# Read-outs and updates in a pair's last step, features formed in PSUM as a minimum, and another order of the mixer's tiles

## The chip, the core and the metric

The kernel runs on one NeuronCore of a Trainium2 chip. Its engines are TensorE (PE, with its weight loads shown apart as PEld), VectorE (DVE), ScalarE (ACT), GpSimd (POOL) and SyncE (SP), which here issues all DMAs in one queue. The metric is the device time of one execution in microseconds (us); lower is better. The median before is that of three runs.

## The reference

Two kinds of layer alternate over x of 2048 rows and 640 columns, in float32: attention (A), mixer (B), attention, mixer, each added to x after a layernorm. Cut to what matters:

```python
def _A_ref(x, wq, wk, wv, wo, beta):        # 32 heads of 20, 4 segments of 512 rows
    phi = lambda t: jnp.where(t > 0, t + 1.0, jnp.exp(t))
    for s in range(N):                      # M, z: the memory of the segments before
        logits = jnp.einsum("bhqd,bhkd->bhqk", qs, ks) * scale + mask   # keys at or before the query
        p = _softmax(logits, axis=-1)
        a_dot = jnp.einsum("bhqk,bhkd->bhqd", p, vs)
        pq = phi(qs)
        num = jnp.einsum("bhld,bhde->bhle", pq, M)
        den = jnp.einsum("bhld,bhd->bhl", pq, z)[..., None] + 1e-6
        o = g * num / den + (1.0 - g) * a_dot
        pk = phi(ks)
        M = M + jnp.einsum("bhld,bhle->bhde", pk, vs)
        z = z + jnp.einsum("bhld->bhd", pk)
    return o @ wo

def _B_ref(x, w_in, w_sp, b_sp, w_out):
    z = _gelu(x @ w_in); z1 = z[..., :864]; z2 = _layernorm(z[..., 864:])
    g = jnp.einsum("ts,bsf->btf", w_sp, z2) + b_sp[None, :, None]
    return (z1 * g) @ w_out
```

The mask in the reference adds -1e9 where the column is after the row.

## The kernel before

**Numbers.** Every float32 operand of a matmul is split into two float16 parts, high and low, by a ScalarE copy and a VectorE subtraction, and each product takes three matmuls (high x high, high x low, low x high).

**Order of work.** For each of the two layers there are three stages: `phase1a` (attention), `phase1b` (the mixer's input side) and `phase2` (its spatial product and its output). TensorE's order is the order in which the code is written. The order on the other engines and in SP's queue is laid out by a planner, from its own estimate of times and from priorities: an operation goes to its engine's queue when the planner thinks that it can start, and `high_priority` puts it ahead of others that can start as well. On the chip each queue then runs strictly in that order.

**`phase1a`.** The heads go in pairs, 16 pairs in each of four segments, 64 in all, and a pair takes three steps (`run`, time t; LEAD steps come before). In each step `scores` computes one chunk of the pair's transposed logits (`es`, read by ScalarE's exponential into P) and one chunk of a later pair's logits (`mp`, read by VectorE's maximum into `mx`), each in one buffer of PSUM. The three chunks have 512, 512 and 256 columns, so a pair's last step (t % 3 == 2) is the lightest. At t % 3 == 0 the maxima of a pair are transposed (`maxes`: matmul `mtp` into the bank "ms", read by ScalarE and then by VectorE into `mr`). `pvs` does P times V for one head at t % 3 == 2 and for the other at t % 3 == 0. `cast` splits P: ScalarE makes the high part, GpSimd the low one.

Between them run the projections (`unit` for q and k, `value`, `project`), cut into pieces that `PACE` deals out in units a step. Each group of them has one of two PSUM banks "dn". When a q or k projection `ps` is done, `out` posts its evacuation to later steps: `parts` one step later (ScalarE and VectorE split it, L701 and L705, and ScalarE takes its exponential, L704), `features` a step after that (a minimum with 1 and a scale, in SBUF, L711, then max(ps, 0) plus that, L713, into `phq` or `phk`), and for keys `keys` a third step later (the split of `phk`, L722 and L723, and a transposing DMA). A step 4 later or more, `update` multiplies the keys with the values into the memory `mst` (matmuls `mup`, bank "ms"). `read` multiplies the queries' features with `mst` (matmuls `num`, bank "ms"); its `out` divides, L760 to L764, into `gm`, one step later. A layer has 18 reads (segments 1 to 3, one for each block of six heads or less) and 15 updates (segments 0 to 2, one for each block of 128 features). The bank "ms" has one buffer, so `mtp`, `num` and `mup` take turns in it. Reads stand at the steps of the list `rd`, and updates are moved on by `post` while

```python
        while free and (t % 3 == 0 or t in self.rd):
            t += 1
```

holds.

**`phase1b`.** For each of 16 tiles of 128 rows: take x1, the rows after the attention (tiles 0 to 11 were projected in `phase1a` and are loaded; tiles 12 to 15 are projected here, from x in `xt` and the attention's output in `o`, by `yp`, L272, and added, L275), layernorm, split, a transposing DMA to `th`, the two halves of w_in (`zp`, L295), gelu and layernorm of the second half (`z2`, split into `zh` and `zl`, L301 to L304), gelu of the first, stored (`z1`). Layernorm of a tile is written one tile ahead, loads two tiles ahead. The buffers of this stage are in pools, one after the other in memory: b2 (`z1`), b1 (`z2`), bx2 (`xt`), bx1 (`o`), bs (staging of w_in, layer 1 only), be2 (`x1`, `th`), be1, bw0 (first half of w_in). `g.wi[0].made` is false in layer 1 and true in layer 2, when the split weights are loaded ready-made.

**`phase2`.** It lies over the same memory: c1 (`u`, `un`, `ut`: 3456, 3584 and 3584 bytes a partition), cr (`wr`, 8192 bytes), ch (`wn`), c2, cw (w_u), cx, ctr (`wt`). For each tile of w_sp, `rows` loads 128 rows (`wr`, L353), takes their largest magnitude (L355), scales and splits them (`wn`, L365 and L366) and transposes them by DMA (`wt`, L367). `spatial` multiplies `wt` with `zh` and `zl`, over k from 0 to 15 (L378), `tail` multiplies by w_out. `rows(0)` is written first, with the priority HP. A tile of `z2` takes 3456 bytes a partition, one of `xt`, `o`, `x1` 2560, one of `z1` 3456.

Of the kernel before, what the change touches and what calls it, by code (L numbers as in the profile page):

```python
# [19 lines left out]
L = S // NSEG  # L20
# [214 lines left out]
def phase1b(g, o_d, x, x1_d, z1_d, zh, zl):  # L235
    nc, tc = g.nc, g.tc
    with ExitStack() as ctx:
        pool = lambda n, b, **k: ctx.enter_context(tc.tile_pool(name=n, bufs=b, reuse_waits="tile", **k))
        p2, p1, px2, px1, sp = pool("b2", 2), pool("b1", 3 if g.wi[0].made else 1), pool("bx2", 2), pool("bx1", 1), pool("bs", 2)

# [41 lines left out]
        def xn_t(xn):  # L282
            th = pe2.tile([128, 2, KD, 128], F16, tag="th", name="th")
            hl = pe1.tile([128, 2, D], F16, tag="xnhl", name="xnhl")
            split_t(g, hl, th, xn)
            return th[:, 0], th[:, 1]
# [19 lines left out]
        def z1_half(t, zp):  # L306
            z1 = p2.tile([128, FH], F32, tag="z1", name="z1")
            nc.scalar.activation(z1.rearrange("p (n c) -> p n c", n=2), zp[:, :, :FHH], AF.Gelu_apprx_tanh, scale=g.zi[0])
            nc.sync.dma_start(z1_d[t], z1)

        with tc.high_priority(offset=HP2):
            a = load(0)
            xn = attn_out(0, *a)
            a = load(1)
            th = xn_t(xn)
        for t in range(NT):
            if t + 1 < NT:
                xn = attn_out(t + 1, *a)
            z2_half(t, w_in_half(1, *th))
            if t + 2 < NT:  # L320
                a = load(t + 2)
            th1 = xn_t(xn) if t + 1 < NT else None
            z1_half(t, w_in_half(0, *th))
            th = th1
# [197 lines left out]
class Attention:  # L522
# [23 lines left out]
    def post(self, k, f, free=False):  # L546

        if self.now is None:
            f()
            return  # L550
        t = self.now + max(k, 1)
        while free and (t % 3 == 0 or t in self.rd):
            t += 1
        self.later.setdefault(t, []).append(f)
# [137 lines left out]
    def out(self, nm, s, m, ps):  # L692

        g, nc = self.g, self.nc
        q = nm == "q"
        ph = []

        def parts():
# [8 lines left out]
            if feature:  # L707
                self.soon(lambda: features(e))

        def features(e):  # L710
            nc.vector.tensor_scalar(e, e, 1.0, g.gq if q else g.gk, ALU.min, ALU.mult)  # L711
            ph.append((self.u4 if q else self.u1).tile([128, L], F32, tag=f"ph{nm}", name=f"ph{nm}"))
            nc.vector.scalar_tensor_tensor(ph[0], ps, 0.0, e, ALU.max, ALU.add)  # L713
            if q:
                self.phq[m] = ph[0]
                self.held["q", m] = s
            else:
                self.soon(keys)

        def keys():  # L720
            hl = self.u2.tile([128, 2, L], F16, tag="hl", name="phl")
            nc.scalar.mul(hl[:, 0], ph[0], g.sig)  # L722
            nc.vector.scalar_tensor_tensor(hl[:, 1], ph[0], g.sig, hl[:, 0], ALU.mult, ALU.subtract)  # L723
            pk = self.u2.tile([128, 2, 4, 128], F16, tag="pk", name="pk")
# [218 lines left out]
    def run(self, nseg=NSEG):  # L943
# [5 lines left out]

        rd = [(G * s + 9 * m - 5 + c0 // 2, s, m, c0) for s in range(1, nseg) for m in range(NU) for c0 in range(0, len(UH[m]), 6)]  # L950
        self.rd = {t for t, _, _, _ in rd}
# [8 lines left out]
        U, V = 6480, 4530  # L960
        PACE = (-LEAD, 2400), (0, 720), (51, 1150), (128, 1250), (END + G, 0)
        order = "02 03 v4 04 v5 v6 v7 10 11 12 13 14 v8 v9 v10 v11 20 21 p0 22 23 24 v12 v13 v14 v15 30 31 p1 32 p2 33 p3 34 p4 p5 p6 p7 p8 p9 p10 p11".split()
# [16 lines left out]
        for c in order:  # L979
# [13 lines left out]
            else:  # L993
# [3 lines left out]
                for r in range(i, i + 1 + (i % NU < NU - 1)):  # L997
                    assert r < NU or beg > G * (r // NU) + 9 * (r % NU) - 4 + (3 if r % NU == 4 else 0), (s, m, r, beg)
                assert step(acc + w) < G * s + 9 * m - LEAD - 3, (s, m, step(acc + w))
# [150 lines left out]
```

## Time and profile before

| | |
|---|---|
| median of 3 runs | 2553.36 us (2547.65 to 2554.88) |
| the profiled execution | 2541.92 us, of which the profile's span is 2540.2 us |
| attention, layers 1 and 2 | about 91 to 698 and 1365 to 1946 us of the span |
| mixer's input side, layers 1 and 2 | about 698 to 906 and 1946 to 2136 us |
| spatial part, layers 1 and 2 | about 913 to 1310 and 2154 to 2540 us |
| busy share | PE 89%, PEld 53%, DVE 57%, ACT 45%, POOL 37% |

A row of the profile names the line of the code, the engine, the operation, the tile written and the tiles read, with partitions x elements and type. In brackets or after a bar stands the idle time of the engine just before, and what ended it ("<-DVE mr L892": the VectorE operation of line 892 that writes `mr`). A busy TensorE is one with a matmul in its pipeline. The granted clock is 1.00 at full speed.

### The profile page before, as it was taken

To read this page: it belongs to the slowest core of one execution; us is meant where nothing else is said; L and a number is where in the kernel's file an instruction comes from. 1 tells how busy PE (TensorE), PEld (TensorE's weight loads), DVE (VectorE), ACT (ScalarE), POOL (GpSimd) and SP (SyncE) were. 2 spreads that over 40 slices of the span, in tenths; PEclk is the share of its full clock that TensorE was granted. 3 is DMA by queue.
4 is the path that set the end of the run, shared out by engine and by line. 5 is a ranking of instruction groups with operands and counts; after the bars stand their busy time and mean duration, and the time that the engine had idled before them with its cause. 6 is when DMAs were issued, how large, how long until landed. Compare 5 with 4: busy or idle time off the path is not lost. (4 is left out here: it accounts for less than half of the span.)

```text
span 2540.2 us, 50727 instructions
## 1 busy us (share of the span) xinstructions
PE 2248.7 (89%) x20682; PEld 1335.2 (53%) x20682; DVE 1451.8 (57%) x2766; ACT 1141.3 (45%) x1388; POOL 946.9 (37%) x728
## 2 busy tenths in 40 slices
PE   3787787899889989999997778879998997999998
PEld 2354454556545545555554445455664553555555
DVE  8667777676655455544336766766766443454431
ACT  3287676677643232212125766657765222211210
POOL 3176676788621000000004767667875100000000
PEclk9999999999999999999999989889999998999999
DMA  6823543434553478766446243342445335577652
GB/s 201 204 62 82 153 117 98 97 91 118 142 161 87 113 209 197 186 162 168 98 117 140 70 104 77 98 97 68 122 125 143 100 98 162 140 190 174 144 143 63
DMA packets 502506, 325.00 MB, mean 128 GB/s; under 512 B 408512, under 2 KB 443456, under 8 KB 497152
## 3 DMA queue, kind: packets, MB, share of 16 engines
q1 hardware_dynamic: 502272, 321.76, 49.2%
q8 instruction: 162, 2.65, 0.4%
q14 instruction: 72, 0.59, 0.1%
HBM read 148.25 MB, written 85.34 MB: 92 GB/s over the span
## 5 line engine op out<-in xcount | busy, mean ns | idle before, releaser
L882 POOL TENSOR_TENSOR PL<-P,PH 128x1280 f16<-128x1280 f32 x248 | 651.7, 2628 | 227.2 <-ACT PH L881 180.7
L871 DVE TENSOR_REDUCE mx<-mp 128x2 f32<-128x1024 f32 (+3 forms) x512 | 408.8, 816 | 180.3 <-PE mp L827 178.5
L378 PE MATMUL gp<-zh,wt 128*128 128x432 f16 x2048 | 466.0, 348 | 27.6 <-DMA wt<-wn 27.6
L864 ACT ACTIVATE P<-es,sc 128x1024 f32<-128x1024 f32 (+1 forms) x384 | 371.2, 967 | 203.4 <-PE es L827 202.3
L378 PEld LDWEIGHTS <-wt 128*128 128x128 f16 x3072 | 301.8, 98 | 289.5 <-DMA wt<-wn 28.9
L881 ACT CAST PH<-P 128x1280 f16<-128x1280 f32 x256 | 320.7, 1254 | 19.6 <-PE pv L908 13.0
L295 PEld LDWEIGHTS <-th 128*128 128x128 f16 x1920 | 188.3, 98 | 167.0 <-issue 4.0
L378 PE MATMUL gp<-zl,wt 128*128 128x432 f16 x1024 | 272.5, 348 | 0.0
L393 POOL MEMSET un<- 128x64 f16 x32 | 4.9, 152 | 672.2 <-DMA ut<-un 618.1
L205 POOL TENSOR_TENSOR lnrs<-lnve,mhalf 128x1 f32<-128x1 f32 x96 | 58.8, 621 | 459.9 <-DVE lnve L204 443.8
L855 PEld LDWEIGHTS <-qk 60*128 60x128 f16 (+1 forms) x2048 | 89.6, 95 | 255.6 <-issue 153.3
L855 PE MATMUL mp<-qk 60*128 60x512 f16 (+3 forms) x1024 | 140.3, 311 | 72.4 <-DVE mx L871 70.3
L355 DVE TENSOR_REDUCE am<-wr 128x1 f32<-128x2048 f32 x32 | 73.1, 2286 | 216.6 <-DMA wr<-in_B_w_sp_dram 216.6
L381 ACT ACTIVATE u<-gp,bsp,un 128x864 f32<-128x864 f32 x32 | 34.2, 1070 | 357.9 <-PE gp L378 345.6
L630 PE MATMUL vps<-wvh,xt 128*128 128x320 f16 x640 | 160.7, 317 | 22.4 <-DMA xt<-xnhl 12.9
L407 PE MATMUL cyp<-wuh,ut 128*128 128x320 f16 (+1 forms) x896 | 166.5, 303 | 8.8 <-DMA ut<-un 8.8
L908 PE MATMUL pv<-vs,PL 128*128 128x41 f16 x2560 | 165.0, 182 | 7.9 <-POOL PL L882 7.3
L908 PE MATMUL pv<-vs,PH 128*128 128x41 f16 x2560 | 168.5, 183 | 3.8 <-DVE ab L924 2.0
L827 PEld LDWEIGHTS <-big 64*128 64x128 f16 x3072 | 142.9, 97 | 52.9 <-issue 3.8
L407 PEld LDWEIGHTS <-ut 128*128 128x128 f16 (+1 forms) x1344 | 132.7, 99 | 66.2 <-DMA ut<-un 10.0
L855 PE MATMUL es<-qk 64*128 64x512 f16 (+3 forms) x1024 | 136.5, 303 | 27.2 <-ACT P L864 21.8
L908 PEld LDWEIGHTS <-PH 128*128 128x128 f16 x2560 | 142.6, 97 | 22.6 <-ACT PH L881 3.1
(181 smaller groups left out, 4152.4 us busy)
## 6 DMA issues: line engine op xcount, KB each, us to landing
wr<-in_B_w_sp_dram SPq DMA_DIRECT2D x32, 1024.0 KB
qk<-st SPq DMA_DIRECT2D x256, 120.0 KB
x<-x SPq DMA_DIRECT2D x56, 320.0 KB
z<-z SPq DMA_DIRECT2D x32, 432.0 KB
cz<-z SPq DMA_DIRECT2D x32, 432.0 KB
xt<-in_A_x_dram SPq DMA_DIRECT2D x32, 320.0 KB
st<-qhl SPq DMA_DIRECT2D x40, 256.0 KB
st<-khl SPq DMA_DIRECT2D x40, 256.0 KB
```

The lines of the kernel that those rows point to most:

```text
L295: nc.tensor.matmul(zp[:, n, :FHH], a[:, k, :], b[:, k, c:c + FHH], start=(k == 0 and j == 0), stop=(k == KD - 1 and j == 2))
L355: nc.vector.tensor_reduce(am, wr, AX.X, ALU.max, apply_absolute_value=True)
L378: nc.tensor.matmul(gp[:, n, :FHH], wt[:, k // 8, a, k % 8, :], b[:, k, n * FHH:(n + 1) * FHH], start=(k == 0 and j == 0), stop=(k == NT - ...
L407: nc.tensor.matmul(yp[:, n, :320], a[:kn[k], k, :], b[:kn[k], k, n * 320:(n + 1) * 320], start=(k == 0 and j == 0), stop=(k == KO - 1 and ...
L630: nc.tensor.matmul(ps, a[:, k, c], b[:, k, n * 320:(n + 1) * 320], start=(i == 0), stop=(i == 14))
L827: nc.tensor.matmul(out, g.big[r, 64 - 64 * s:192 - 64 * s], mk, start=False, stop=s == 1, skip_group_check=True)
L855: nc.tensor.matmul(out[:, h, o:o + w], a[r, ac], b[r, bc], start=o == 0, stop=False, skip_group_check=True)
L864: nc.scalar.activation(P[:, :, 512 * c:512 * c + ew], es[:, :, :ew], AF.Exp, scale=g.esc)
L871: nc.vector.tensor_reduce(self.mx[m][:, :, i], mp[:, :, o:o + w], AX.X, ALU.max)
L881: nc.scalar.copy(PH, P[:, h])
L882: (nc.gpsimd if h == 0 or n < self.N - self.TAIL else nc.vector).tensor_tensor(PL, P[:, h], PH, ALU.subtract)
L908: nc.tensor.matmul(pv[:, i, h, :], x[:, c:c + 128], v[:, j, h0 + h, :], start=(j == 0 and x is PH), stop=(j == i and x is PL), skip_group_ ...
```

## The change

It has four parts.

1. In `phase1b` the tiles are taken in the order 0 to 7, 12 to 15, 8 to 11, so that the four with projections stand in the middle. In layer 2, `z2` has one buffer instead of three and `o` three instead of one.
2. `features` goes. In `parts`, VectorE replaces `ps` in PSUM by max(ps, 0) + c (c is the scale of 1), and takes the minimum of that and the exponential times c: for t > 0 the exponential is not below t + 1, for t <= 0 it is not above 1. For a query the result goes to `phq`, for a key back into `ps`. `keys` comes one step later instead of two, and reads PSUM. The tile `phk` (2048 bytes) is gone.
3. Reads move one step later, from t % 3 == 1 to the pair's last step, and updates are allowed only there, at a step that has no read.
4. `PACE` deals out 700 units a step up to step 53 instead of 720 up to step 51.

```diff
-        p2, p1, px2, px1, sp = pool("b2", 2), pool("b1", 3 if g.wi[0].made else 1), pool("bx2", 2), pool("bx1", 1), pool("bs", 2)
+        p2, p1, px2, px1, sp = pool("b2", 2), pool("b1", 1), pool("bx2", 2), pool("bx1", 3 if g.wi[0].made else 1), pool("bs", 2)
...
+        ts = [*range(NWO - 4), *range(NWO, NT), *range(NWO - 4, NWO)]
         with tc.high_priority(offset=HP2):
-            a = load(0)
-            xn = attn_out(0, *a)
-            a = load(1)
+            a = load(ts[0])
+            xn = attn_out(ts[0], *a)
+            a = load(ts[1])
             th = xn_t(xn)
-        for t in range(NT):
-            if t + 1 < NT:
-                xn = attn_out(t + 1, *a)
+        for i, t in enumerate(ts):
+            if i + 1 < NT:
+                xn = attn_out(ts[i + 1], *a)
             z2_half(t, w_in_half(1, *th))
-            if t + 2 < NT:
-                a = load(t + 2)
-            th1 = xn_t(xn) if t + 1 < NT else None
+            if i + 2 < NT:
+                a = load(ts[i + 2])
+            th1 = xn_t(xn) if i + 1 < NT else None
             z1_half(t, w_in_half(0, *th))
...
-        while free and (t % 3 == 0 or t in self.rd):
+        while free and (t % 3 < 2 or t in self.rd):
...
             if feature:
-                self.soon(lambda: features(e))
-
-        def features(e):
-            nc.vector.tensor_scalar(e, e, 1.0, g.gq if q else g.gk, ALU.min, ALU.mult)
-            ph.append((self.u4 if q else self.u1).tile([128, L], F32, tag=f"ph{nm}", name=f"ph{nm}"))
-            nc.vector.scalar_tensor_tensor(ph[0], ps, 0.0, e, ALU.max, ALU.add)
-            if q:
-                self.phq[m] = ph[0]
-                self.held["q", m] = s
-            else:
-                self.soon(keys)
+                one = g.gq if q else g.gk
+                nc.vector.tensor_scalar(ps, ps, 0.0, one, ALU.max, ALU.add)
+                ph = self.u4.tile([128, L], F32, tag="phq", name="phq") if q else ps
+                nc.vector.scalar_tensor_tensor(ph, e, one, ps, ALU.mult, ALU.min)
+                if q:
+                    self.phq[m] = ph
+                    self.held["q", m] = s
+                else:
+                    self.soon(keys)
...
-            nc.scalar.mul(hl[:, 0], ph[0], g.sig)
-            nc.vector.scalar_tensor_tensor(hl[:, 1], ph[0], g.sig, hl[:, 0], ALU.mult, ALU.subtract)
+            nc.scalar.mul(hl[:, 0], ps, g.sig)
+            nc.vector.scalar_tensor_tensor(hl[:, 1], ps, g.sig, hl[:, 0], ALU.mult, ALU.subtract)
...
-        rd = [(G * s + 9 * m - 5 + c0 // 2, s, m, c0) for s in range(1, nseg) for m in range(NU) for c0 in range(0, len(UH[m]), 6)]
+        rd = [(G * s + 9 * m - 4 + c0 // 2, s, m, c0) for s in range(1, nseg) for m in range(NU) for c0 in range(0, len(UH[m]), 6)]
...
-        PACE = (-LEAD, 2400), (0, 720), (51, 1150), (128, 1250), (END + G, 0)
+        PACE = (-LEAD, 2400), (0, 700), (53, 1150), (128, 1250), (END + G, 0)
```

More of the change, by code (lines that the diff above doesn't have):

```diff
@@ L695, in out @@
         q = nm == "q"
-        ph = []
         def parts():
@@ L997, in run @@
                 for r in range(i, i + 1 + (i % NU < NU - 1)):
-                    assert r < NU or beg > G * (r // NU) + 9 * (r % NU) - 4 + (3 if r % NU == 4 else 0), (s, m, r, beg)
+                    assert r < NU or beg > G * (r // NU) + 9 * (r % NU) - 3 + (3 if r % NU == 4 else 0), (s, m, r, beg)
                 assert step(acc + w) < G * s + 9 * m - LEAD - 3, (s, m, step(acc + w))
```

## The prediction

> **What bounds the kernel now.** I read the page first, then the busy time by stage, then TensorE's waits, and last the chain of work at the places that these named.
>
> ```profile
> span 2540.2 us, 50727 instructions
> PE 2248.7 (89%) x20682; PEld 1335.2 (53%) x20682; DVE 1451.8 (57%) x2766; ACT 1141.3 (45%) x1388; POOL 946.9 (37%) x728
> ```
>
> TensorE carries the kernel; no other engine is above 57%. So the question is where TensorE stands still. The stages (start:end in us, length, then PE, PEld, DVE, ACT, POOL busy with counts, clock, DMA share, GB/s), here attention and mixer of layer 1, of layer 2, and a gap before layer 2's spatial part:
>
> ```profile
> 91.00:698.00 607.00, 508.70 (x6735) 317.44 (x6732) 427.90 (x807) 415.80 (x523) 418.46 (x275) 0.95 0.43 111
> 698.00:906.00 208.00, 197.63 (x1197) 109.40 (x1194) 104.19 (x206) 67.14 (x75) 31.37 (x39) 0.98 0.45 121
> 1365.00:1946.00 581.00, 492.40 (x6666) 310.39 (x6664) 396.80 (x753) 405.41 (x500) 421.91 (x278) 0.94 0.38 98
> 1946.00:2136.00 190.00, 188.70 (x1069) 103.95 (x1069) 88.65 (x188) 55.14 (x63) 22.39 (x35) 0.98 0.36 93
> 2136.00:2155.00 19.00, 0.81 (x4) 0.28 (x3) 6.34 (x9) 3.17 (x3) 0.15 (x1) 0.60 0.96 317
> ```
>
> The mixer is full (188.7 of 190), the attention stages leave 98 and 89 us, and 18 us are empty at 2136. What ended TensorE's waits (total, times, longest):
>
> ```profile
> PE mp L855 <- DVE mx L871: 70.3, 59, 3.5
> PE num L751 <- DVE mr L892: 46.3, 26, 3.3
> PE mup L781 <- DVE mr L892: 29.5, 13, 3.8
> PE gp L378 <- DMA wt<-wn: 27.6, 3, 18.2
> ...
> PE kps L687 <- DVE phk L713: 10.8, 4, 2.9
> ```
>
> Nearly all are waits for VectorE: for the maxima of the chunk before (`mx`), for `mr`, which empties the one PSUM bank "ms" that transposed maxima, read-outs (`num`) and updates (`mup`) share, and 27.6 us for the first rows of w_sp.
>
> **Part 1, the mixer's order and its buffers.** The rows of the first spatial tile go wr load, maximum, wn, transposing load to wt. In layer 2 (chain) and at both starts (TensorE):
>
> ```profile
> 2069.26 10.95 PE zp L295 x60
> 2136.27 0.32 SPq L96
> 2137.17 7.06 DMA wr<-in_B_w_sp_dram
> 2144.26 2.30 DVE am L355
> 2149.84 4.54 DMA wt<-wn
> 913.03 0.90 PE L378 MATMUL gp<-zh,wt 128*128 128x432 f16 x2 [7.44 <-DMA wt<-wn]
> 917.91 0.53 PE L378 MATMUL gp<-zl,wt 128*128 128x432 f16 x2
> 918.28 0.89 PE L378 MATMUL gp<-zh,wt 128*128 128x432 f16 x4
> 935.00 0.54 PE L378 MATMUL gp<-zh,wt 128*128 128x432 f16 x2 [1.96 <-DMA wt<-wn]
> 2154.43 0.90 PE L378 MATMUL gp<-zh,wt 128*128 128x432 f16 x2 [18.19 <-DMA wt<-wn]
> ```
>
> The whole chain, 17.3 us, lies open in layer 2. By the tile sizes, added up in the order of the pools, wr takes bytes 10,624 to 18,816 of the stage. In layer 1 these are xt and o of the projected tiles, in layer 2 the second and third z2 and the first xt. Layer 1's queue shows it: wr is issued the moment the last projected tile has been added.
>
> ```profile
> 883.73 0.89 DVE L275 SCALAR_TENSOR_TENSOR x<-yp,sc,xt 128x640 f32<-128x640 f32 x1 [3.38 <-PE yp L272]
> 884.64 0.33 SPq L353 DMA_DIRECT2D wr<-in_B_w_sp_dram  x1
> 2119.85 0.98 ACT L301 ACTIVATE z<-zp,sc 128x864 f32<-128x864 f32 x1 [1.13 <-PE zp L295]
> 2124.90 1.06 DVE L304 TENSOR_TENSOR zl<-z,zh 128x864 f16<-128x864 f32 x1 [1.03 <-ACT zh L303]
> ```
>
> In layer 2 tile 14's z2 is free at 2125.96, but wr stands in SP's queue behind the load of w_u (L96), whose memory w_in holds until TensorE's last matmul. After the change only xt and o lie under wr in both layers (z2 ends at 10,368 with one buffer, three o end at 23,168), and both are free five tiles, 5 x 10.95 = 55 us, before the mixer's end. The chain of 17.3 us then fits with room, even for wn's second half, which lies on the x1 buffer freed some two tiles (22 us) before the end. Gain: 7.44 + 1.96 in layer 1, 18.19 in layer 2, and the slow clock after each gap: 14 matmuls took 4.88 us (913.03 to 917.91) where 0.18 us apiece makes 2.6, so 2.3 us each. Sum 32 us. Ends: 0, if another load keeps wr back, and 32.
>
> The projections themselves only move: 60 matmuls in 10.95 us per tile stay, the last tile's zl is now needed at the twelfth of sixteen k instead of the sixteenth, 12 us into the spatial tile, so nothing waits. One z2 buffer in layer 2 is free: its life, 2119.85 to 2125.96, is 6.1 us of a tile's 10.95, as in layer 1 now. The x1 stores, loads of xt and transposing loads of o keep their number and stand four iterations earlier in SP's queue, the x1 loads of tiles 8 to 11 four later; the wr load and the two wt transposes are moved ahead of the last tiles' th transposes, which have a tile's time of cover. Maximum and two splits, 2.3 + 2 x 1.28 us of VectorE, go into a stage where it is busy 88.65 of 190 us. If that cover failed, the price is one th late by these 4.9 us a layer.
>
> **Part 2, features in PSUM.** Groups (count, busy us, mean ns, idle before) and one line's spread (min/median/max):
>
> ```profile
> L711 DVE TENSOR_SCALAR eq<-eq,sc 128x512 f32<-128x512 f32 x60 | 57.3, 956 | 0.0
> L723 DVE SCALAR_TENSOR_TENSOR phl<-phk,sc,phl 128x512 f16<-128x512 f32 x30 | 35.7, 1189 | 2.3 <-ACT phl L722 2.2
> L713 DVE SCALAR_TENSOR_TENSOR phq<-qps,eq 128x512 f32<-128x512 f32 x30 | 20.7, 691 | 0.3
> L711 DVE TENSOR_SCALAR eq<-eq,sc x60: 465/838/2608, 78.3 to 1843.0; 128x512 f32<-128x512 f32 x60
> ```
>
> Operations that read a projection in PSUM take 0.69 us, all alike; the two that read only SBUF scatter up to 2.6 us. The count of operations stays; L711's successor and L723 now read PSUM. A one-input operation from PSUM to PSUM is not in the trace: ends 0.465 (the fastest L711) and 0.956 (no change); I take 0.69, the nearest row. Then 57.3 - 60 x 0.69 = 15.9, and 35.7 - 30 x 0.69 = 15.0: 30.9 us less VectorE. How much of it TensorE sees depends on how often a scattered one stands before `mx` or `mr`; ends 0 and 31, I take half, 15.5. The features no longer wait a step for the exponential, but their first operation stands behind L705, which needs ScalarE's split; the exponential is issued next to that split, so I cost the wait at nothing, and at one more ScalarE operation of L705's size each (60 x 0.69 = 41, not in the sum) if another stands between.
>
> A key's bank is now held until L723, two more operations on it, about 2 x 0.69 = 1.4 us, against four known waits for `phk` (10.8 us): 4 x 1.4 = +5.6, ends 0 and 30 x 1.4 = 42. A query's bank is free a step earlier.
>
> **Part 3, read-outs and updates in step 3 of a pair.** One read-out that waited, one that did not, and what follows each:
>
> ```profile
> 1473.08 1.75 DVE L711 TENSOR_SCALAR eq<-eq,sc 128x512 f32<-128x512 f32 x1
> 1475.88 1.28 DVE L871 TENSOR_REDUCE mx<-mp 128x2 f32<-128x768 f32 x2
> 1477.08 0.27 DVE L892 SCALAR_TENSOR_TENSOR mr<-mtp,mr 8x128 f16<-8x128 f32 x1
> 1477.40 1.96 PE L751 MATMUL num<-mst,phq 128*128 128x126 f32 x8 [3.35 <-DVE mr L892]
> 1480.02 0.66 DVE L764 TENSOR_TENSOR gm<-num,den 128x480 f32<-128x480 f32 x1
> 1792.80 1.16 PE L751 MATMUL num<-mst,phq 128*128 128x126 f32 x8
> 1795.97 0.38 PE L687 MATMUL kps<-xt,wkl 128*128 128x512 f16 x1
> 1797.36 0.39 PE L855 MATMUL mp<-qk 60*128 60x512 f16 x2
> 1798.58 0.27 PE L889 MATMUL mtp<-ident,mx 128*8 128x128 f32 x1
> ```
>
> Today a read-out comes one step after the maxima's transpose (`mtp`), ahead of that step's projections, and waits for `mr`, which VectorE takes late. In the last step it comes after the projections, the third chunk's scores and a P.V product, which fill the wait. But `mr` stands just behind the middle chunk's `mx` (1475.88), and the third chunk's scores wait for that too: most of the wait turns into a wait for `mx`. Of 46.3 + 29.5 = 75.8 us I take a third, 25; ends 0 and 75.8. After long waits matmuls run slower: the eight of a read-out 1.96 against 1.16. About six such waits spared, with the projections behind them some 1.3 us each: 8; ends 0 and 39 x 1.3 = 51.
>
> Late next is `mtp`, which finds the bank still read by `gm`: the read-out's three VectorE operations end 1480.68, 1.3 us after the matmuls (1479.36), and TensorE has 1795.97 to 1798.58 = 2.6 us of other work before `mtp`. Covered unless VectorE is busy: 36 read-outs x 0.4 = +14; ends 0 and, with a 1.22 us `mx` and its wait for scores put first, 1.7 x 36 = 61. An update moved to the last step may start up to three steps later; its state is read only a segment later.
>
> **Part 4, pace.** By step 128 the projections have had 53 x 700 + 75 x 1150 = 123,350 units instead of 51 x 720 + 77 x 1150 = 125,270; at 1250 a step they end 1.5 steps later, some 190 of 200. The ten steps left cover it: 0. Without them, 1.5 x 2.8 us a layer.
>
> **The sum.** -32 - 15.5 + 5.6 - 25 - 8 + 14 = -60.9 us. The profiled execution took 2541.92 us (span 2540.2), so 2481; the median of the runs shown is 2553.36, 0.45% higher, and 2553 - 61 gives 2492, my forecast for a median.
>
> **Rivals.**
> (a) The attention gains nothing: each wait for `mr` becomes one for `mx`. For it: `mx` is already the largest row. 2553 - 32 = 2521.
> (b) Fp32 from PSUM costs a rate. The fastest L711 needs 0.465 us, an operation on PSUM 0.69: if the 0.465 were what matters, part 2 would lose 60 x 0.225 = 13.5 and win 15.0 back on L723, net 0; 2492 + 15.5 = 2508. The median of 838 ns speaks against it. The Trainium skill, "VectorE: DVE Perf Modes", section "Why PSUM operands drop a tier", states that an operation that doubles its rate on two SBUF read ports loses that with a PSUM operand; the trace agrees on the ends, but not on the mean.
> (c) The first spatial tile still waits, because a load placed before wr holds SP's queue: 2553 - 29.5 = 2524. Layer 2 shows just that now; against it, the memory is free so much earlier.
> (d) All of it counts: VectorE's 31 us, two thirds of the `mr` waits (50), the clock 20, no new waits: 2553 - 133 = 2420.
> (e) Slower: the "ms" bank. VectorE takes the `mx` of the next pair before the read-out's division, so `mtp` waits 1.7 us at all 36 read-outs (+61), and since `mr` is then late too, nothing of the 25 and the 8 comes: -32 - 15.5 + 5.6 + 61 = +19, 2572. It decides from about 1.4 us a read-out.
> (f) Neither hand-over nor attention moves: 2553.
>
> **How the numbers follow.** Chances: forecast 0.39, (a) 0.20, (b) 0.06, (c) 0.10, (d) 0.10, (e) 0.09, (f) 0.06. The forecast's own range is 2470 to 2510; with (a), (b), (c) and a share of (d) it becomes 2445 to 2532. Faster by over 0.3% (about 8 us, what a measurement can tell): 0.39 + 0.20 + 0.06 + 0.10 + 0.10 = 0.85; same 0.06; slower 0.09.
>
> **What would show it.** Part 1: no TensorE wait for wt over 1 us, the wr load issued some 50 us before the mixer's end. Part 2: the feature operations at 0.65 to 0.75 us without scatter. Part 3: `num` and `mup` almost gone from the waits for `mr`, a new small row of `mtp` waiting for `gm`, and `mx` shrunk or grown: if it has grown by what `mr` lost, (a) holds. The forecast fails if wr is still behind w_u, if `mtp <- gm` is over 40 us, or if `phk`'s row grows by tens.

## The result, and the profile after

The changed kernel took 2469.86 us (median of 4 runs, 2468.54 to 2476.31) against 2550.51 us (4 runs, 2545.8 to 2554.88) of the kernel before on the same chip: a ratio of 0.9689, 95% interval 0.9662 to 0.9716, or 81 us less. The prediction said 2492 in a range of 2445 to 2532. The sum came out near by luck, not by its own terms: the mixer's order, which was to bring the most, brought nothing, and the attention brought far more, so that two errors of opposite sign largely cancelled. The profiled executions give the same picture (spans 2540.2 and 2466.8 us).

The busy time of the changed kernel's engines, and what ended TensorE's waits (total us, times, longest):

```profile
PE 2224.2 (90%) x20682; PEld 1317.4 (53%) x20682; DVE 1431.5 (58%) x2766; ACT 1137.3 (46%) x1388; POOL 937.1 (38%) x728
```

```profile
PE mp L855 <- DVE mx L871: 55.0, 72, 3.2
PE es L855 <- ACT P L864: 34.7, 44, 2.2
PE kps L689 <- DVE phl L723: 25.6, 6, 8.3
PE gp L380 <- DMA wt<-wn: 23.8, 4, 12.2
...
PE es L855 <- DMA qk<-mr: 10.2, 7, 3.5
```

The rows for `mr` (46.3 of the read-outs, 29.5 of the updates) are gone but for 0.5, and `mx` has shrunk with them, from 70.3 to 55.0. Three rows have grown: the key projections that wait for their bank (10.8, now 25.6), the scores behind P and behind their queries (21.8 and 3.6, now 34.7 and 10.2). The wait for wt has hardly moved (27.6, now 23.8). Together the rows for `mr`, `mx`, the key projections and the scores fall by 57 us.

Busy time by stretch shows where that ends up (start:end, length, PE, PEld, DVE, ACT, POOL with counts, clock, DMA share, GB/s). First before, then after, cut in each layer at the first scores, at the last chunk of logits for a maximum (below: the attention's end; the last pair's own scores still follow it), at the first projection of the mixer and at the first spatial product:

```profile
97.00:687.00 590.00, 492.38 (x6577) 308.02 (x6577) 420.58 (x795) 407.28 (x513) 412.29 (x270) 0.95 0.42 111
687.00:698.50 11.50, 10.82 (x148) 6.85 (x144) 5.27 (x10) 8.32 (x10) 6.68 (x6) 0.76 0.41 81
698.50:913.00 214.50, 197.13 (x1181) 108.90 (x1177) 108.61 (x210) 70.31 (x79) 30.87 (x39) 0.97 0.46 126
1335.00:1923.00 588.00, 498.19 (x6576) 310.94 (x6576) 405.11 (x779) 400.17 (x501) 412.71 (x276) 0.94 0.40 101
1923.00:1933.50 10.50, 8.58 (x145) 5.92 (x140) 5.41 (x10) 8.10 (x10) 8.04 (x6) 1.00 0.50 89
1933.50:2154.40 220.90, 197.52 (x1181) 108.99 (x1177) 100.97 (x203) 64.39 (x72) 30.11 (x40) 0.95 0.42 121
```

```profile
100.50:652.00 551.50, 486.76 (x6556) 302.40 (x6556) 409.17 (x790) 403.48 (x510) 407.49 (x270) 0.96 0.44 116
652.00:670.00 18.00, 13.83 (x202) 9.04 (x202) 11.11 (x18) 12.40 (x14) 9.69 (x8) 0.91 0.46 113
670.00:878.50 208.50, 195.36 (x1144) 107.32 (x1140) 105.85 (x206) 67.04 (x76) 27.60 (x37) 0.99 0.46 128
1301.00:1836.00 535.00, 473.57 (x6557) 296.60 (x6556) 386.68 (x763) 395.87 (x499) 408.33 (x274) 0.99 0.41 105
1836.00:1866.80 30.80, 14.83 (x252) 10.41 (x251) 16.94 (x34) 16.01 (x17) 17.23 (x15) 0.82 0.49 156
1866.80:2073.50 206.70, 194.51 (x1080) 106.44 (x1080) 94.39 (x193) 58.23 (x66) 18.98 (x30) 0.96 0.45 113
```

Read as differences: the two attention stretches lose 38.5 and 53.0 us, 91.5 in all. Of these 61 are idle time (187.4 before, 126.2 after: length less PE) and 30 are busy time of TensorE on about the same count of matmuls, at a clock of 0.96 and 0.99 instead of 0.95 and 0.94. The two stretches behind them must be read together, because work moves across the cut between them: in layer 1 the mixer is 6.0 us shorter and the stretch ahead of it 6.5 longer (226.0 us in sum before, 226.5 after); in layer 2 it is 14.2 shorter and 20.3 longer (231.4 before, 237.5 after). So these stretches, from which the sum expected most of its first 32 us, give back 6.6. Another 6.9 are given back in the last spatial part (385.6 us before, 392.5 after) and some 3.5 before the first scores; no term of the sum had these.

### The profile page after: what moved, and what is told of

Read it like the earlier page. It is cut to its first block, busy times and chain, and to the rows that moved or that the text cites. A ratio compares the mean times of both kernels' runs of the same rounds, so it can differ in the third digit from the quotient of the medians.

```text
span 2466.8 us, 50722 instructions
## 1 busy us (share of the span) xinstructions
PE 2224.2 (90%) x20682; PEld 1317.4 (53%) x20682; DVE 1431.5 (58%) x2766; ACT 1137.3 (46%) x1388; POOL 937.1 (38%) x728
## 4 chain that ended last, share of the span: by engine, by line
PE 56%; DVE 10%; ACT 10%; DMA 9%; issue 5%; SPq 3%; POOL 3%; ACTq 0%; DVEq 0%; POOLq 0%
PE gp L380 16%; PE zp L295 13%; PE cyp L409 6%; ACT PH L881 3%; ACT P L864 3%; PE vps L632 3%; PE pv L908 3%; DVE mx L871 3%; DMA wr<-in_B_w_sp_dram 2%; PE kps L689 2%; PE mp L855 2%; PE qps L689 2%; PE yps L665 2%; PE es L855 2%; POOL PL L882 2%
## 5 line engine op out<-in xcount | busy, mean ns | idle before, releaser
L380 PE MATMUL gp<-zh,wt 128*128 128x432 f16 x2048 | 466.6, 348 | 23.8 <-DMA wt<-wn 23.8
L881 ACT CAST PH<-P 128x1280 f16<-128x1280 f32 x256 | 320.5, 1253 | 19.2 <-PE pv L908 12.8
L409 PE MATMUL cyp<-wuh,ut 128*128 128x320 f16 (+1 forms) x896 | 166.8, 303 | 11.9 <-DMA ut<-un 11.9
L855 PE MATMUL es<-qk 64*128 64x512 f16 (+3 forms) x1024 | 134.3, 298 | 47.3 <-ACT P L864 34.7
L295 PE MATMUL zp<-wi1h,th 128*128 128x432 f16 x640 | 150.2, 349 | 8.8 <-DMA th<-xnhl 8.8
```

What stands on the lines that cost most here:

```text
L295: nc.tensor.matmul(zp[:, n, :FHH], a[:, k, :], b[:, k, c:c + FHH], start=(k == 0 and j == 0), stop=(k == KD - 1 and j == 2))
L380: nc.tensor.matmul(gp[:, n, :FHH], wt[:, k // 8, a, k % 8, :], b[:, k, n * FHH:(n + 1) * FHH], start=(k == 0 and j == 0), stop=(k == NT - ...
L409: nc.tensor.matmul(yp[:, n, :320], a[:kn[k], k, :], b[:kn[k], k, n * 320:(n + 1) * 320], start=(k == 0 and j == 0), stop=(k == KO - 1 and ...
L855: nc.tensor.matmul(out[:, h, o:o + w], a[r, ac], b[r, bc], start=o == 0, stop=False, skip_group_check=True)
L881: nc.scalar.copy(PH, P[:, h])
```

## Experiments

All ratios are to the kernel before, run beside each kernel on its chip; "us" is the ratio's distance from 1 times 2551. Two kernels are compared by this column, unless the text gives their medians.

| kernel | median us | ratio, 95% interval | us |
|---|---|---|---|
| part 1 alone | 2556.21 | 1.0010 (0.9998 to 1.0023) | +3 |
| part 2 alone | 2506.30 | 0.9820 (0.9795 to 0.9846) | -46 |
| part 3 alone | 2479.55 | 0.9717 (0.9694 to 0.9740) | -72 |
| updates of part 3 alone | 2527.53 | 0.9910 (0.9893 to 0.9927) | -23 |
| read-outs of part 3 alone | 2485.38 | 0.9742 (0.9726 to 0.9757) | -66 |
| parts 2 and 3 | 2464.22 | 0.9668 (0.9644 to 0.9692) | -85 |
| all three (the change) | 2469.86 | 0.9689 (0.9662 to 0.9716) | -79 |
| the change, first operation in SBUF | 2483.53 | 0.9752 (0.9728 to 0.9776) | -63 |
| the change, x1 off the attention's pool | 2462.65 | 0.9667 (0.9645 to 0.9688) | -85 |
| the change, wn and wt lying free | 2434.64 | 0.9543 (0.9524 to 0.9562) | -117 |
| the same, all key features in SBUF | 2438.74 | 0.9575 (0.9554 to 0.9597) | -108 |
| the same, the first key features in SBUF | 2429.42 | 0.9524 (0.9508 to 0.9541) | -121 |
| parts 2 and 3 with pads, order of before | 2455.36 | 0.9625 (0.9609 to 0.9641) | -96 |

### Part 1 alone

```diff
-p2, p1, px2, px1, sp = pool("b2", 2), pool("b1", 3 if g.wi[0].made else 1), pool("bx2", 2), pool("bx1", 1), pool("bs", 2)
+p2, p1, px2, px1, sp = pool("b2", 2), pool("b1", 1), pool("bx2", 2), pool("bx1", 3 if g.wi[0].made else 1), pool("bs", 2)
...
+ts = [*range(NWO - 4), *range(NWO, NT), *range(NWO - 4, NWO)]
```

> Part 1 alone on the kernel before: the mixer's order and its two buffer counts, nothing in the attention. Theory, from the two traces: the load of wr now goes out some 60 us early, but the split wn sits in ScalarE's queue right behind the last tile's zh, so the transposing loads of wt still come after the mixer's last matmul; only wr and the maximum leave the open chain. Expected: layer 1's wait for wt stays at 7 us, layer 2's falls from 18 to about 12, and two to four waits for ut of some 2.7 us come in behind it: 5 to 15 us less in all, about 2541. Rival A (the sum of the prediction): the order alone is worth 32 us and something in the attention's change took it back: 2519. Rival B: the order is worth nothing, because what the second gap loses comes back as waits for ut: 2551.

Measured: +3 us, no difference. Rival B's number, but by another way than it named. TensorE's wait at layer 2's hand-over fell from 18.2 to 12.2 us as the theory said; the stretch from the attention's end to the first projection, before 10.5 us (row 1923.00:1933.50), took 30.7:

```profile
1927.00:1957.70 30.70, 13.45 (x243) 9.74 (x237) 15.51 (x31) 16.02 (x17) 15.50 (x15) 0.72 0.49 155
1957.70:2163.00 205.30, 193.18 (x1080) 106.03 (x1080) 94.41 (x193) 58.22 (x66) 19.01 (x30) 0.97 0.44 114
```

205.3 instead of 220.9 in the mixer, 30.7 instead of 10.5 ahead of it: the order pays 20.2 us in layer 2 to gain 15.6. Part of both is the same work on the other side of the cut, as the mixer's first projections now stand behind the last scores; the sum of the two, 236.0 instead of 231.4, is 4.6 us longer although the wait for wt is 6 us shorter.

### Parts 2 and 3 alone, and together

Part 2 alone is the change's `parts` and `keys`, part 3 alone the two lines below with the pace and the bound on the order of jobs; the third kernel has both.

```diff
-                nc.vector.tensor_scalar(e, e, 1.0, g.gq if q else g.gk, ALU.min, ALU.mult)
+                nc.vector.tensor_scalar(ps, ps, 0.0, one, ALU.max, ALU.add)
```
```diff
-        while free and (t % 3 == 0 or t in self.rd):
+        while free and (t % 3 < 2 or t in self.rd):
-        rd = [(G * s + 9 * m - 5 + c0 // 2, ...
+        rd = [(G * s + 9 * m - 4 + c0 // 2, ...
```

> Part 2 alone on the kernel before: features in the projection's own step, max and add written back to PSUM, min taken from PSUM; read-outs, updates and mixer as before. Theory: VectorE loses 23 us of busy time, of which a third or so reaches TensorE, and the key's bank is held longer, which costs 15 us in waits of the key projections: between -15 and +10 us, taken at -5, 2546. Rival A: the scattered SBUF-only operations were what made mx and mr late, so this part carries the attention's gain: 30 us or more less, with num<-mr and mup<-mr much smaller in the trace, 2520 or less. Rival B: the part costs by itself because of the key bank: 15 us more, 2566.

> Part 3 alone on the kernel before, with the pace that its order of jobs needs: read-outs and updates in the third step of a pair; features and mixer as before. Theory: the waits for mr (75.8 us) go nearly whole, with mx about as before (70) and mtp<-gm under 5: 50 to 65 us less, about 2493. Rival A (the prediction's third): 25 to 35 us less, about 2520, because the scattered feature operations still keep mx late and the waits move there: mx grows by 30 us or more. Rival B: it only works together with the shorter feature operations: under 15 us less.

> Parts 2 and 3 together on the kernel before, with the pace; the mixer's order and buffers as before. Alone, part 2 was worth 46.7 us, part 3 73.4 us and part 1 nothing (-3.2). Theory: parts 2 and 3 take away the same waits for mr, so together they are worth no more than some 80 us, and part 1 is worth nothing beside them either, as its gain of 12 to 15 us in the mixers is lost where layer 2's mixer starts: 2470, within 8 us of the changed kernel. Rival A: part 1 is worth its 15 us or more here, and this kernel takes 2485. Rival B: part 1 costs here too, more than it gains: 2455.

Measured: -46, -72 and -85 us. Part 2 alone met its rival A: it was worth nine times what the theory gave it. Part 3 alone did a little more than the theory, and rival A of it (a third) is out. Together they are worth 85, not 118: each removes waits that the other removes too. TensorE's waits in part 2 alone, then in part 3 alone:

```profile
PE mp L853 <- DVE mx L869: 56.7, 63, 3.5
PE num L749 <- DVE mr L890: 35.2, 28, 2.9
...
PE mup L779 <- DVE mr L890: 7.5, 6, 2.3
```

```profile
PE mp L855 <- DVE mx L871: 87.6, 90, 3.2
```

With shorter features `mr` is in time for three quarters of what the updates waited (29.5 to 7.5) and a quarter of the read-outs (46.3 to 35.2). With the read-outs and updates moved, no row of `num` or `mup` for `mr` is left, and 17 of the 76 us turn up at `mx` (70.3 to 87.6): a quarter, where the prediction had let two thirds turn up there. With both, `mx` is at 58.3. The third kernel is 6 us ahead of the changed kernel, with intervals that overlap (0.9644 to 0.9692 and 0.9662 to 0.9716): part 1 brings nothing beside the others either.

### Updates and read-outs, each alone

The updates alone are this line; the read-outs alone are the other line of part 3, with the pace and the bound on the order.

```diff
-        while free and (t % 3 == 0 or t in self.rd):
+        while free and (t % 3 < 2 or t in self.rd):
```

> One half of part 3 alone on the kernel before: updates go only into the last step of a pair; read-outs stay where they were, a step after the maxima's transpose. Theory: each kind of product saves its own wait for mr: mup's 29.5 us go, num's 46.3 stay: 20 to 30 us less, about 2522. Rival A: most of part 3's 73 us hang on the updates, because an update also holds VectorE's next mr back: 50 us less or more. Rival B: the waits move to num: under 10 us less.

> The other half of part 3 alone on the kernel before: read-outs one step later, in the last step of a pair, with the pace and the bound on the order that this needs; updates still in the second or third step where no read-out stands. Theory: num's 46.3 us go, mup's 29.5 stay, and as the read-outs now fill the third step, more updates stand in the second, so mup's wait grows by up to 10: 35 to 45 us less, about 2510. Rival A: nearly all of part 3 is in the read-outs: 65 us less or more, 2480. Rival B: the waits move to mup: 15 us less or less.

Measured: -23 us, as the theory said, and -66 us, its rival A. TensorE's waits, first with only the updates moved (no row of `mup` for `mr` is left), then with only the read-outs (none of `num`):

```profile
PE mp L855 <- DVE mx L871: 86.3, 74, 3.1
PE num L751 <- DVE mr L892: 42.6, 25, 3.3
```

```profile
PE mp L855 <- DVE mx L871: 66.1, 69, 3.6
...
PE mup L781 <- DVE mr L892: 21.3, 14, 3.6
```

Each move removes its own wait and leaves most of the other's. What differs is `mx` (70.3 before): with the updates moved it takes back 16 of their 29.5 us, with the read-outs moved it falls by 4. So the 17 us that part 3 hands to `mx` come with the updates; the read-outs' wait did not turn into one for `mx`. The read-outs brought 66 us for 46.3 of waiting, and 62 of them lie in the two attention stretches: TensorE stands idle there for 149.4 us instead of 187.4, 38 less and not 46, since the wait for P takes some back (30.1 us instead of 21.8), and it is busy for 966.6 instead of 990.6, 24 less for the same products, at a clock of 0.96 and 0.98 instead of 0.95 and 0.94.

### The first feature operation back in SBUF

```diff
-                nc.vector.tensor_scalar(ps, ps, 0.0, one, ALU.max, ALU.add)
+                nc.vector.tensor_scalar(e, e, 1.0, one, ALU.min, ALU.mult)
-                nc.vector.scalar_tensor_tensor(ph, e, one, ps, ALU.mult, ALU.min)
+                nc.vector.scalar_tensor_tensor(ph, ps, 0.0, e, ALU.max, ALU.add)
```

> The changed kernel with the features in the same step as now, but formed as before: minimum and multiply on the exponential in SBUF, then max and add from PSUM (keys still end in their own bank). One difference: the first operation works in SBUF. Theory: this operation scatters again (mean 0.9 us, up to 2 us and more, where the one in PSUM takes 0.75 at every time), VectorE is busy 8 to 13 us longer, and mx is late more often: 5 to 15 us more than the changed kernel, 2480. Rival A: what counted was that the features come in the step of their projection and the key's split reads PSUM; the place of the first operation is worth nothing: 2470. Rival B: half of these operations then take 0.47 us and no longer wait on nothing else: 5 to 10 us less, 2462.

Measured: 16 us slower than the changed kernel, the theory's upper end; the intervals are apart (0.9728 to 0.9776 and 0.9662 to 0.9716). So the memory of this one operation matters, not only the step it stands in; it is worth no less than what part 2 still adds to part 3 (13 us). The wait for `mx`, 55.0 us in the changed kernel, has grown by 12:

```profile
PE mp L855 <- DVE mx L871: 67.3, 74, 3.2
```

The operation's spread (min/median/max ns), here and in the changed kernel:

```profile
L711 DVE TENSOR_SCALAR eq<-eq,sc x60: 465/630/2047, 77.8 to 1790.9; 128x512 f32<-128x512 f32 x60
```

```profile
L711 DVE TENSOR_SCALAR kps<-kps,sc x30: 737/750/754, 77.8 to 1634.1; 128x512 f32<-128x512 f32 x30
L711 DVE TENSOR_SCALAR qps<-qps,sc x30: 736/749/751, 188.8 to 1769.8; 128x512 f32<-128x512 f32 x30
```

What makes it scatter stands on another engine. Rows of VectorE and GpSimd of this kernel, in order of time:

```profile
1475.59 2.62 POOL L882 TENSOR_TENSOR PL<-P,PH 128x1280 f16<-128x1280 f32 x1
1476.62 1.87 DVE L711 TENSOR_SCALAR eq<-eq,sc 128x512 f32<-128x512 f32 x1
```

GpSimd's split of P ends at 1478.21, the feature operation at 1478.49, 0.28 us later. The same 0.28 to 0.29 us stand behind nearly every split of P that such an operation met halfway, however early it began. I set every such operation of the kernel before beside GpSimd's operations in its trace: 25 of the 60 had none beside them for more than 4 ns and took 465 to 478 ns; the 34 covered for half their time or more took 470 to 2608, 1320 on average. The split of the key's feature with both inputs in SBUF (L723 before) does the same: 734 to 752 ns for the 10 with nothing beside them, up to 2359 for the others. With an operand in PSUM nothing of it is seen: 33 operations of the changed kernel's L711 lay wholly under GpSimd's and took 736 to 751. No run takes GpSimd's work away; the cause rests on these ends and on the operation's move.

The Trainium skill, "SBUF — State Buffer", section "SBUF: two separate sides", says that VectorE and GpSimd share one pair of SBUF ports, and that for a VectorE operation in a two-port mode or with two SBUF inputs it is "an **exclusive lock**, not a bandwidth split", held for a whole instruction by whichever starts first. These rows agree for the operation on `eq`: one that meets the 2.62 us split of P lasts until 0.28 us after the split's end, and the one that began 0.16 us ahead of a split (kernel before, at 301.9 us) took 0.47 us.

### x1 off the attention's pool

```diff
+pad = 168 if g.wi[0].made else 0
-xt = px2.tile([128, D], F32, tag="xt", name="xt")
+xt = px2.tile([128, D + pad], F32, tag="xt", name="xt")[:, :D]
```

> The changed kernel with xt 168 floats wider in layer 2's mixer, and nothing else: that moves x1 from byte 162,272 to 163,616, just past the attention's last pool but one (158,496 to 163,616); wn still lies on x1. Theory: in layer 2 the first loads of x1 waited for that pool (issued at 1849.71, 14 us after the attention's last scores; before, 19 us ahead of them), so the first tile of the mixer no longer fills the attention's end. With the pad the first x1 is loaded before the last scores, the first projections of w_in lie between the last P.V products, the wait of 7.3 us for th goes, and layer 2's stretch from last scores to first spatial tile is 10 to 15 us shorter; the wait for wt stays near 12 us: 10 to 16 us less than the changed kernel, about 2457. Rival A: the late start is the order's own (the queues hold the loads for another reason), and nothing moves: 2470. Rival B: an earlier start is given back in full at the hand-over to the spatial part.

Measured: 6 us less than the changed kernel, half of what the theory said, with intervals that overlap. The trace shows the mechanism and where the rest stayed. SP's queue, first load of x1 of layer 2 in the changed kernel, then with the pad, and then the padded kernel's stretches:

```profile
1849.71 0.83 SPq L254 DMA_DIRECT2D x<-x  x2
```

```profile
1823.94 0.39 SPq L255 DMA_DIRECT2D x<-x  x1
```

```profile
1843.00:1861.00 18.00, 14.19 (x206) 9.16 (x205) 10.99 (x18) 12.55 (x15) 9.69 (x7) 0.91 0.57 177
1861.00:2068.70 207.70, 193.39 (x1141) 106.93 (x1137) 98.15 (x199) 60.85 (x69) 26.49 (x37) 0.98 0.44 115
```

The changed kernel loads x1 14 us after the attention's end, the padded one 19 us ahead of it. From there to the first spatial product it takes 225.7 us instead of 237.5, 11.8 less, as expected; but the attention before it took 541.5 us instead of 535.0 in this build, most of it busy time of TensorE (478.5 instead of 473.6) at a clock of 0.97 instead of 0.99. So the cause of the 30.8 us row is shown (three z2 became one and o three, which put x1 of layer 2 at byte 162,272, on a pool of the attention that ends at 163,616), its worth only as 6 to 12 us.

### wn and wt lying free

```diff
+pad = 480 if g.wi[0].made else 256
-xt = px2.tile([128, D], F32, tag="xt", name="xt")
+xt = px2.tile([128, D + pad], F32, tag="xt", name="xt")[:, :D]
-xo = px.tile([128, 2, 320], F32, tag="xo", name="xo")
+xo = px.tile([128, D + 32], F32, tag="xo", name="xo")[:, :D].rearrange("p (n c) -> p n c", n=2)
```

> The changed kernel, with its buffers shifted by padding and nothing else: xt of the projected tiles is 480 (layer 2) or 256 (layer 1) floats wider and xo 32 floats, so that wn (bytes 157,920 to 166,112) no longer lies on x1's buffers, and wt's first buffer no longer on w_in's. Every instruction and its operands stay. Theory: what kept the hand-over was wn's memory, not the order. wn and the two transposing loads of wt then leave the queues while the last tiles of the mixer run, TensorE has no wait for wt over 1 us in either layer: 15 to 25 us less than the changed kernel, about 2449. Rival A: the transposing loads still come late, because the transposes of the last tiles' th and the stores before them hold the queue or collide with them: th is late by 5 us a layer and the gain is under 8 us, 2464. Rival B: the time comes back behind the hand-over as waits for ut and cx1, because the first spatial tiles then catch up with the load of w_u: under 5 us less, 2467.

Measured: 35 us less than the changed kernel by the medians (2434.64 against 2469.86; 37 by the ratios), more than the theory's 15 to 25, and 4.6% less than the kernel before. The pad also moves x1 off the attention's pool, so the 11.8 us of the experiment before are part of it; whether wn's buffer or wt's held the chain was not told apart. The hand-over in layer 2, all engines, in the changed kernel:

```profile
1996.83 0.34 SPq L355 DMA_DIRECT2D wr<-in_B_w_sp_dram  x1
...
2060.26 0.91 ACT L303 CAST zh<-z 128x864 f16<-128x864 f32 x1 [3.13 <-DVE z L211]
2061.08 2.18 ACT L367 ACTIVATE wn<-wr,ivw 128x1024 f16<-128x1024 f32 x2
2061.61 0.32 SPq L96 DMA_DIRECT2D wuh<-w_uh  x1
2064.36 9.50 SPq L369 DMA_TRANSPOSE wt<-wn  x2
2073.81 0.90 PE L380 MATMUL gp<-zh,wt 128*128 128x432 f16 x2 [12.22 <-DMA wt<-wn]
```

wr is loaded 64 us ahead of the mixer's end, as predicted, and its maximum taken at 2002.2; then nothing of the chain follows until wn, which stands in ScalarE's queue right behind the last zh. With the pads, the waits for wt are gone from TensorE's list, and the first spatial product comes without one:

```profile
1976.93 0.34 SPq L356 DMA_DIRECT2D wr<-in_B_w_sp_dram  x1
2032.86 3.93 SPq L370 DMA_TRANSPOSE wt<-wn  x1
...
2042.23 0.53 PE L381 MATMUL gp<-zh,wt 128*128 128x432 f16 x2
```

wn's first half now runs at 1987.5, 74 us earlier than at 2061.1. By stretches, layer 1's mixer falls from 208.5 to 200.4 and its spatial part from 422.5 to 414.5, layer 2's end of attention from 30.8 to 18.0 and its mixer from 206.7 to 195.8, the last part from 392.5 to 390.2; layer 2's attention took 543.3 instead of 535.0, with 61.7 and 61.4 us of idle time in it: the 8 us are busy time (481.6 and 473.6) at a clock of 0.97 instead of 0.99.

### The same pads without the mixer's order

```diff
-xt = px2.tile([128, D], F32, tag="xt", name="xt")
+xt = px2.tile([128, D + 256], F32, tag="xt", name="xt")[:, :D]
```

> Parts 2 and 3 with the mixer's order and buffer counts of before, and the same kind of pads (xt 256 floats wider in both layers, xo 32): wn no longer lies on x1, wt no longer on w_in, but wr still lies on buffers that the last tiles use. Without the pads this took 2464.2. Theory: order and memory are needed together in layer 2. There wr still stands behind the load of w_u and the wait of 18 us for wt stays; in layer 1, where wr is free one tile before the end, the wait of 7.4 us and the one behind it go, with the slow clock after them: 10 to 15 us less than without the pads, 2452. Rival A: the memory alone was the obstacle: 25 us less or more, 2438. Rival B: without the order the pads do nothing in either layer: 2464.

Measured: 9 us less than without the pads by the medians (2455.36 against 2464.22; 11 by the ratios), near the theory's 2452. In layer 1 the wait for wt is 1.13 us, where the kernel before has 7.44; in layer 2 it stays:

```profile
870.12 0.54 PE L378 MATMUL gp<-zh,wt 128*128 128x432 f16 x2 [1.13 <-DMA wt<-wn]
...
2064.60 0.90 PE L378 MATMUL gp<-zh,wt 128*128 128x432 f16 x2 [18.16 <-DMA wt<-wn]
```

The order alone brings nothing (+3), the pads alone 9 to 11, order and pads 32 (0.9668 to 0.9543): in layer 2 it takes both.

### The key's feature in SBUF, for all keys or for the first

On the kernel with wn and wt free:

```diff
-ph = self.u4.tile([128, L], F32, tag="phq", name="phq") if q else ps
+ph = self.u4.tile([128, L], F32, tag="phq", name="phq") if q else self.e1.tile([128, L], F32, tag="phk", name="phk")
```
and in the second kernel the new tile only while `self.now is None or self.now < 0`, else `ps`.

> The last kernel of the first set (changed kernel with its buffers shifted so that wn and wt lie free, 2434.6) with the key's feature written to SBUF instead of back into its bank, so that a key's PSUM bank is free one operation after the other instead of after its split. Theory: the waits of the key projections for that split (27.7 us, of it two of 9 us at the start of each layer's attention) fall to some 10, but the split (0.74 us from PSUM) takes up to 1.19 us from SBUF, 13 us more VectorE: 5 to 12 us less, 2427. Rival A: the start's waits are those of the queue of transposes behind them and stay, with VectorE longer: 5 us more, 2440. Rival B: no change, 2435.

> The changed kernel with its buffers shifted (2434.6), and the key's feature in SBUF only for the keys formed before the first pair; all others end in their bank. Theory: in each layer the wait of some 9 us of the key projections at the start falls to about 3, as where all keys went to SBUF (attention began at 96.6 instead of 100.8 us), and the later splits keep 0.74 us: 4 to 8 us less, 2429. Rival A: what is gained at the start is waited for by the maxima behind it: no change, 2435.

Measured: 2438.74, 4 us more than with all keys in their bank by the medians (8 by the ratios), rival A's end; and 2429.42, 5 us less, the theory's number. Both intervals overlap that of the kernel they start from (0.9554 to 0.9597, and 0.9508 to 0.9541, against 0.9524 to 0.9562), so neither difference is certain. With all keys in SBUF their wait falls (27.7 to 12.8), but the split takes 735 to 2766 ns and `mx` grows from 56.7 to 76.7:

```profile
PE mp L856 <- DVE mx L872: 76.7, 83, 3.5
...
PE kps L690 <- DVE phk L714: 12.8, 4, 5.9
```

```profile
L724 DVE SCALAR_TENSOR_TENSOR phl<-phk,sc,phl x30: 735/1392/2766, 81.4 to 1634.9; 128x512 f16<-128x512 f32 x30
```

With SBUF for the first keys alone the wait falls as far (12.8), the eight splits from SBUF take 732 to 752 ns with no GpSimd operation beside them, and `mx` grows only to 64.1: the gain stays, and about a third of the price. That kernel has the lowest median here.

## Why the prediction was right in sum and wrong in its terms

**Part 1, -32 predicted, nothing measured.** The step that failed is "The chain of 17.3 us then fits with room, even for wn's second half, which lies on the x1 buffer freed some two tiles (22 us) before the end". I had worked out wr's bytes against the buffers above it and found them free five tiles early, and they were. But a chain is only as early as its last buffer: wn was still planned behind the last tile's zh, and its transposing loads then stood behind w_u's loads, so of the chain only wr and the maximum went, 6 of the 18.2 us in layer 2; with wn's and wt's buffers moved it all went. And I had costed the moved pools at nothing outside the mixer: x1 of layer 2 slid onto a pool that the attention still used, which cost 12 us (237.5 against 225.7) at the place where the mixer's first tile used to fill the attention's end. The 32 us themselves were sized about rightly: against parts 2 and 3 without the order, order and pads together brought 32, with all 29.8 us of waiting for wt gone. That this agrees to the microsecond is chance, since the attention stretches of these builds differ by several. Rival (c), "The first spatial tile still waits", was the nearest, with another holder than the one it named.

**Part 2, -15.5 + 5.6 = -10 predicted.** On top of part 3 it brought 13 (0.9717 to 0.9668), alone 46. The durations were taken at 0.69 and came to 0.745 (L711) and 0.741 (L723), and L713 rose from 0.687 to 0.741, so VectorE lost 22.8 us instead of 30.9 (57.3 + 35.7 + 41.2 before; 44.7 + 22.2 + 44.5 after). Counting half of that time was too low by far: alone, the part brought twice the busy time that VectorE lost. I read that so, that an operation which meets GpSimd comes late just where `mx` and `mr` stand behind it in VectorE's queue; that is argued from the rows, and only the 16 us of the one operation, with 12 more of waiting for `mx`, are measured. The bank's price was +14.8 instead of +5.6 (25.6 against 10.8): not 1.4 us at each known wait, but up to 8.3 us at a layer's start. Rival (b), that fp32 from PSUM costs a rate, is right on the rate (0.745 us against 0.47 alone in SBUF) but falls on the time, with the operation put back into SBUF: 16 us slower.

**Part 3, -25 - 8 + 14 = -19 predicted.** On top of part 2 it brought 39 (0.9820 to 0.9668), alone 72. The mis-sized term is "most of the wait turns into a wait for `mx`": a quarter did, and that quarter came with the updates; with the read-outs alone `mx` fell. The +14 for `mtp` behind `gm` came to 1.2 us (1.9 with part 3 alone), so the 2.6 us of cover held and rival (e) had no ground. The clock's 8 came to some 30 us of busy time over all parts. For the attention rival (d) was nearest: its terms there make 101 us, and the two stretches lost 91.5.

**Part 4.** Its own worth was not tried: the read-outs' new place needs it. The stretch behind the attention's end is 18.0 us instead of 11.5 and 10.5 even where x1 is loaded in time, but nothing is lost by that: the mixer's first projections now stand behind the last pair's scores (layer 1: scores until 669.5 us, projection from 670.4) and not among them (before: projection from 698.5, scores until 706.3), and the mixer's own stretch is shorter by about as much. In layer 2 the stretch is 18.1 us with the read-outs alone (with the pace), 10.8 with the updates alone and 11.9 with part 2 alone; whether the read-outs or the pace moved the projections was not told apart.

So -32 that did not come and some -50 that were not foreseen left a total 20 us under the forecast. What stays open besides: why the granted clock of an attention stretch differs from build to build (0.99 and 0.97 in layer 2 for the same edit with and without pads, worth 8 us), and why the last spatial part is 6.9 us longer.

## What to carry to other kernels

An operation of VectorE that, like these two, reads and writes only SBUF may be priced by what GpSimd does at that moment, not by its fastest row: look at its spread, set the slow ones beside GpSimd's rows, and give it a PSUM operand where a bank can be spared. Before a hand-over is counted, follow every buffer of its chain to the byte, and after pools are resized do the same for the stage ahead, since the buffers that slide may fall on memory that is still in use. And parts that remove the same wait must not be added: two that brought 46 and 72 us alone brought 85 together.

## What the hardware showed that was not expected

- VectorE blocked, not slowed, by GpSimd: 0.47 us alone, up to 2.6 us beside the split of P, ending 0.28 us after it.
- An operation with one input from PSUM back to PSUM, 128x512 fp32, takes 0.745 us, at 736 to 754 ns for all 60.
- TensorE's products took less time in kernels where it waited less: in the two attention stretches 990.6 us busy and 187.4 idle before, 966.8 and 139.2 with part 3 alone, 960.3 and 126.2 after, at about the same count of matmuls. It is no strict rule: with the first operation back in SBUF it is 974.6 and 131.6.
